# A new job list for a one-core spectral filter kernel: other order of the loads, other division of the evictions

## The chip, the core and the metric

The kernel runs on one core of a Trainium2 chip. Its time is the device time of one execution in microseconds (us); of several executions the median is given. Beside it stands one execution that the hardware profiler recorded; every duration of a single instruction comes from that one. The engines are TensorE (PE in the profile, its weight loads PEld), VectorE (DVE), ScalarE (ACT), GpSimd (POOL) and SyncE (SP), which only issues transfers. ACT and POOL issue transfers too. All transfers share 16 DMA engines.

## The reference

Two filters are applied to the same `x` (2048 x 1024, bf16). Each is a real two-dimensional FFT, a product with complex weights of 2048 x 513, and the inverse FFT. A gate, one number per row of `x`, mixes the two results.

```python
def _A_ref(x, w_r, w_i):
    B, S, D = x.shape
    X = rfft2(x.astype(float32), axes=(-2, -1))
    W = w_r + 1j * w_i
    X = X * W
    return irfft2(X, s=(S, D), axes=(-2, -1)).astype(bfloat16)
# _B_ref is the same with its own weights
g = sigmoid((x * gate_w).sum(-1, keepdims=True))
return g * _A_ref(x, A_w_r, A_w_i) + (1 - g) * _B_ref(x, B_w_r, B_w_i)
```

`B_x` is an input and is not used.

## The kernel before, in words

The transforms are cut into small DFTs that are matrix products with constant tables. The work runs in these stages; each has a name for its matmuls (ending in m) and one for the copy of the result out of PSUM (ending in e), which is called an eviction.

- **Loads.** `load.x.g.dh`: `x` comes in eight groups g, each in two halves of 256 KB. Tables: `load.E` (two parts), `F2`, `CK`, `U5`, `DI`, a 2 KB table of signs `SM`. `load.W.h.b.m.f` brings the weights of filter f for column half h and blocks b to b+m-1; each is four transfers.
- **s1 (groups 0 to 7, two column halves j).** `egen.c.v` makes signed copies of table E (v = 1 and 3 multiply with SM on DVE, 2 negates on ACT). `fold.g.k` adds, subtracts (groups 0 to 3) or reverses (groups 4 to 7) columns of `x` on DVE. `s1m.g.j` is 8 matmuls, `s1e.g.j` the eviction into buffer FR. Every later stage needs all sixteen of these evictions.
- **s2 and s4 (pairs p = 0 to 7, halves h = 1, then 0).** `s2m`, `s2e`, `s4m`, `s4e`; then `swap.p.h`, two transfers that exchange odd and even partitions of the result, and `xneg.p.h`, which multiplies the result with signs and must come after the swap has landed.
- **prod.t.h.c (t = 0 to 15, t = 2p and 2p+1).** The product with both filters' weights, on DVE. For h = 1 there are sixteen whole products. For h = 0, t = 0 to 9 are whole (c = 2); t = 10 to 15 are cut into two half products, c = 0 and c = 1. A weight block can be loaded only when the products that read the block before it in the same place are done.
- **s5 (g = 0 to 31).** `s5m.16` to `s5m.31` need all products of h = 1. `s5m.8` to `s5m.15` need the whole products of h = 0 and the halves c = 1; `s5m.0` to `s5m.7` need the whole ones and the halves c = 0. `s5e` evicts.
- **s6 and s7 (the way back).** `s6m.p.h` needs all `s5e` of its h, and table U5 scaled by the gate (`rb`, `al`). `s7m.i` (i = 0 to 15), `s7c` (ACT copies half of the result), `s7p` (two DVE additions), `fin` (two additions per i on DVE or POOL), `store`. For i = 14 and 15 the `s7p` write the output themselves and there is no `fin`.
- **The gate** beside it: `gsm`, `gse`, `rowsum`, `stm`, `zsm`, and `zse`, a sigmoid on ACT. `sig0` is a sigmoid of zeros whose only use is that it comes before. `warm` and `keep` are matmuls on zeros.

PSUM has four units of 1024 columns; a stage's matmuls take one, and its eviction gives it back.

What sets the order is a long string, `ORDER`: jobs in the order in which they are recorded. The last letter of a job names its engine or queue (a ACT, d DVE, p POOL, s SP). `Prog.add` appends each instruction to its engine's list, and derives the waits from the keys that it reads and writes. On every engine the instructions run strictly in the order of the list; nothing is reordered later. Eviction, sign, negation and addition have a helper each (lines 313 to 337), so that one line of the profile collects many jobs: L317 is every copy on ACT, L319 every copy on DVE, L322 every product, L326 and L328 signs on ACT and DVE, L332 negations on ACT, L337 every matmul, L313 every transfer, L472 the additions of `fold`, L753 `s7p`, L759 `fin`, L667 `sig0`. FR, WP and WR are the SBUF buffers, PS is PSUM.

Of the kernel before, what the change touches and what calls it, by code (L numbers as in the profile page):

```python
# [26 lines left out]
load.W.1.2.2.0.s fold.4.0.d fold.0.0.d s1m.7.0 s1m.7.1 s1m.3.1 s1e.1.1.a s1m.4.1 load.CK.s load.W.1.2.2.1.s fold.0.1.d s1e.7.0.a s1m.0.0
s1e.7.1.a s1e.3.1.a s1m.4.0 s1e.4.1.d s1m.0.1 s1m.3.0 load.R.1.0.1.1.s load.W.1.0.1.0.s s1e.0.0.a s1e.4.0.d s1m.1.0 s1e.0.1.a s1e.1.0.a
s1e.3.0.d load.GR.a keep.5.2 s2m.7.1 s2m.5.1 s2e.7.1.d s2e.5.1.d s2m.4.1 s4m.7.1 s4m.5.1 s2m.0.1 s2e.4.1.d rev s4e.7.1.a swap.7.1.a
s4e.5.1.d swap.5.1.a load.W.1.0.1.1.s s2m.6.1 s4m.4.1 s2e.6.1.d s2m.3.1 s4e.4.1.a s4m.6.1 swap.4.1.s s2e.0.1.d s2e.3.1.a s2m.1.1 s4m.3.1  # L30
xneg.7.1.d prod.14.1.2.d gwm s4e.6.1.a xneg.5.1.d load.W.1.1.1.1.s s2e.1.1.a s4e.3.1.a s4m.0.1 load.R.1.0.1.0.p load.W.1.1.1.0.s
prod.15.1.2.d gwe.a s4e.0.1.a prod.10.1.2.d xneg.4.1.d w5.0.a w5.2.a s2m.6.0 prod.11.1.2.d gsm.12.2 s2e.6.0.a swap.6.1.p gsm.8.2 s4m.1.1
prod.9.1.2.d gse.12.2.a s4e.1.1.a xneg.6.1.d load.VC.s s2m.2.1 swap.1.1.s gsm.10.2 gse.8.2.a prod.8.1.2.d prod.13.1.2.d s2e.2.1.a s4m.6.0
gse.10.2.a gsm.4.2 s4e.6.0.a swap.3.1.p prod.12.1.2.d gse.4.2.a keep.1.2 xneg.1.1.d gsm.6.2 xneg.3.1.a s4m.2.1 prod.6.1.2.d swap.0.1.p
gse.6.2.a prod.3.1.2.d gsm.0.2 w5.1.a s4e.2.1.a xneg.0.1.a swap.6.0.s gse.0.2.a w5.3.a s2m.4.0 s2m.0.0 s2m.5.0 s2e.4.0.a s2e.0.0.a gsm.14.2
gse.14.2.a s4m.4.0 prod.2.1.2.d s2e.5.0.a s4e.4.0.a prod.1.1.2.d s4m.0.0 s4m.5.0 gsm.2.2 s4e.0.0.a gse.2.2.a s2m.2.0 s2m.1.0 swap.2.1.s
prod.0.1.2.d xneg.6.0.d rowsum.0.d s4e.5.0.a prod.7.1.2.d load.W.0.2.2.1.s xneg.2.1.d rowsum.1.d s2e.2.0.a load.W.0.2.2.0.s s2e.1.0.a stm
prod.5.1.2.d swap.4.0.p load.W.0.0.1.0.s s2m.7.0 s2m.3.0 ste.a xneg.4.0.d s4m.1.0 load.W.0.0.1.1.s swap.0.0.p load.R.0.0.1.1.p prod.4.1.2.d
s4m.2.0 s2e.7.0.a s4m.7.0 xneg.0.0.d s2e.3.0.a s4e.1.0.a s4e.2.0.a s4e.7.0.a prod.8.0.2.d stx.s s5m.24 prod.12.0.0.d swap.5.0.p s5m.30
load.R.0.0.1.0.p s4m.3.0 s5e.24.a s5e.30.a rowsum.2.p stp.2.d swap.1.0.s keep.8.2 swap.7.0.s s5m.23 prod.13.0.0.d prod.9.0.2.d stp.0.d  # L40
s5m.16 swap.2.0.s keep.10.2 zsm load.W.0.1.1.1.s s4e.3.0.a prod.0.0.2.d keep.3.2 s5e.16.a xneg.1.0.d s5e.23.a s5m.31 keep.4.2 zse
prod.1.0.2.d xneg.7.0.d xneg.5.0.a s5m.27 s5e.27.a s5m.19 s5m.17 swap.3.0.p s5e.31.a prod.12.0.1.d xneg.2.0.d prod.14.0.0.d load.W.0.1.1.0.s
s5m.29 prod.11.0.0.d s5m.28 s5e.17.a prod.3.0.2.d prod.10.0.0.d keep.7.2 s5m.20 s5e.29.a s5m.21 s5e.28.a s5m.18 xneg.3.0.a s5e.19.a
prod.2.0.2.d keep.9.2 s5e.21.a stp.1.d keep.11.2 s5m.26 s5m.22 s5e.18.a zst.p keep.0.2 prod.5.0.2.d prod.4.0.2.d prod.15.0.0.d keep.2.2
prod.7.0.2.d keep.6.2 prod.6.0.2.d prod.13.0.1.d s5e.20.a s5e.26.a prod.14.0.1.d s5m.25 s5m.2 prod.11.0.1.d prod.15.0.1.d s5e.22.a c0m s5m.4
s5e.25.a s5m.1 s5e.2.a zld.s load.U5.s prod.10.0.1.d c0e.a rb.0.p s5e.4.a s5m.5 s5e.1.a s5m.3 s5m.0 s5e.5.d s5m.8 s5m.12 s5e.3.a s5e.0.d
# [789 lines left out]
```

## Time and profile before

| | us |
|---|---|
| median of 3 runs | 132.87 (132.73 to 132.93) |
| profiled execution, its own time | 132.51 |
| its span, first to last instruction | 130.7 |
| PE busy | 109.0 |
| DVE busy | 105.1 |
| ACT busy | 92.5 |
| POOL busy | 48.8 |
| mean granted TensorE clock | 0.961 |

The span is 1.8 us shorter than the profiled execution's time; what lies around it is start and end of the program. No engine is busy throughout, so shares of the span say little. The stages have different bounds: loads of `x` until 20 us, then a stretch to 91 us in which PE, ACT, DVE and the transfers feed each other, then s6 and s7. A row of the timeline gives the start, the duration, engine, line, operation, buffers, shape, count, and in brackets the idle time before it and what ended it. A row of the chain of waits gives start, duration and what the time was spent on. A row of a windows view gives the stretch, its length, each engine's busy time with the number of instructions, the granted TensorE clock, the DMA share and GB/s.

### The profile page before, as it was taken

The numbers are of one execution on the slowest core, as the hardware profiler recorded it, in microseconds if no ns is written. First come the engines' busy times: TensorE is split into PE (matmuls) and PEld (weight loads), VectorE is DVE, ScalarE is ACT, GpSimd is POOL, SyncE is SP. The second block draws the span as 40 slices with busy tenths as digits, with TensorE's granted clock in tenths as the row PEclk, the third lists the DMA queues.
The fourth block names the chain that finished last, engine by engine and source line by source line (L and its number), as shares of the span: only waits on it lengthen the run. The fifth ranks groups of instructions, "written<-read, shape, count | busy, mean of one in ns | idle before, by whom it ended". The sixth has DMA issues, their size and how long they took to land.

```text
span 130.7 us, 3713 instructions
## 1 busy us (share of the span) xinstructions
PE 109.0 (83%) x1553; PEld 87.0 (67%) x1553; DVE 105.1 (80%) x135; ACT 92.5 (71%) x121; POOL 48.8 (37%) x58
## 2 busy tenths in 40 slices
PE   6964997899999969979987835999999987999900
PEld 3343876668677756927675525999999986798300
DVE  0216858698999699973999799799979999999990
ACT  0750696521999599998999982999388995679110
POOL 3000000012170002950310000999345894999480
PEclk9997799999999999999999996799999999999995
DMA  3899999978689729999756784600000312174347
GB/s 85 284 351 351 365 327 331 294 167 209 214 222 302 245 90 242 276 346 303 230 183 176 203 271 153 291 0 5 5 0 0 115 50 86 75 278 170 115 151 259
DMA packets 27507, 25.56 MB, mean 196 GB/s; under 512 B 2834, under 2 KB 23074, under 8 KB 27234
## 3 DMA queue, kind: packets, MB, share of 16 engines
q1 hardware_dynamic: 22544, 18.41, 47.4%
q10 hardware_dynamic: 3714, 3.95, 8.9%
q0 software_dynamic: 1232, 2.96, 6.3%
q8 instruction: 12, 0.20, 0.7%
q14 instruction: 5, 0.04, 0.1%
HBM read 16.90 MB, written 4.20 MB: 161 GB/s over the span
## 4 chain that ended last, share of the span: by engine, by line
PE 37%; DMA 20%; DVE 14%; ACT 8%; SPq 7%; issue 6%; ACTq 4%; DVEq 1%
PE PS L337 37%; DMA WP<-in_A_x_dram 9%; DVE WP L322 8%; DMA WR<-in_A_w_i_dram 7%; SPq L313 7%; ACTq L313 4%; ACT WP L317 4%; DVE FR L753 4%; DMA WP<-WP 3%; ACT FR L317 2%; DVE WP L472 1%; ACT L667 1%; ACT WP L332 1%; DVEq L775 1%; DVE WR L753 0%
## 5 line engine op out<-in xcount | busy, mean ns | idle before, releaser
L317 ACT ACTIVATE WP<-PS 128x1024 bf16<-128x1024 f32 (+1 forms) x51 | 49.1, 1019 | 15.2 <-PE PS L337 14.9
L317 ACT ACTIVATE FR<-PS 128x1024 bf16<-128x1024 f32 (+1 forms) x44 | 36.2, 890 | 12.3 <-PE PS L337 9.2
L337 PE MATMUL PS<-FR,WP 128*128 128x128 bf16 (+2 forms) x384 | 32.6, 246 | 1.3 <-DVE FR L753 1.0
L337 PEld LDWEIGHTS PS<-FR,WP 128*128 128x128 bf16 x384 | 28.4, 130 | 5.1 <-DVE FR L753 1.4
L337 PE MATMUL PS<-CK,WP 128*128 128x64 bf16 x512 | 20.2, 202 | 5.4 <-DVE WP L322 4.7
L337 PEld LDWEIGHTS PS<-CK,WP 128*128 128x128 bf16 x512 | 19.3, 119 | 8.0 <-DVE WP L322 5.3
L759 POOL TENSOR_TENSOR WR<-FR 128x512 bf16<-128x512 f32 x15 | 20.4, 1369 | 7.5 <-DVE FR L753 7.2
L319 DVE CAST WP<-PS 128x1024 bf16<-128x1024 f32 x14 | 16.5, 1218 | 3.4 <-PE PS L337 3.3
L753 DVE TENSOR_TENSOR FR<-PS,FR 128x512 f32<-128x512 f32 x28 | 17.7, 678 | 1.2 <-ACT FR L317 1.0
L322 DVE TENSOR_TENSOR WP<-FR,WR 128x1024 bf16<-128x1024 bf16 (+1 forms) x18 | 14.6, 866 | 3.1 <-issue 2.2
L337 PE MATMUL PS<-F,FR 128*128 128x128 bf16 x256 | 15.9, 219 | 1.2 <-ACT FR L317 0.6
L337 PEld LDWEIGHTS PS<-F,FR 128*128 128x128 bf16 x256 | 14.7, 98 | 3.1 <-ACT FR L317 1.6
L337 PE MATMUL PS<-WP 128*128 128x256 bf16 (+1 forms) x128 | 13.4, 265 | 3.8 <-DMA WP<-in_A_x_dram 2.7
L337 PEld LDWEIGHTS PS<-WP 128*128 128x128 bf16 x128 | 10.6, 106 | 6.9 <-DMA WP<-in_A_x_dram 3.5
L322 DVE TENSOR_TENSOR WP<-WP,WR 128x2048 bf16<-128x2048 bf16 x12 | 14.3, 1217 | 0.0
L337 PE MATMUL PS<-FR 128*128 128x480 bf16 (+3 forms) x52 | 11.7, 364 | 2.7 <-ACT WP L317 1.4
L322 POOL TENSOR_TENSOR FR<-FR,F 128x1024 bf16<-128x1024 bf16 x3 | 7.3, 2438 | 16.0 <-DMA FR<-c_U 16.0
L759 DVE TENSOR_TENSOR WR<-FR 128x512 bf16<-128x512 f32 x13 | 12.6, 990 | 0.0
L313 POOL DMA_DIRECT2D FR<-FR x8 | 4.5, 565 | 17.9 <-PE PS L337 17.9
L577 POOL COPY FR<-FR 128x128 bf16<-128x128 bf16 x1 | 0.3, 292 | 27.3 <-DMA FR<-c_RG 27.3
L337 PE MATMUL PS<-WP,CK 128*128 128x512 bf16 (+4 forms) x44 | 8.7, 328 | 0.0
L337 PEld LDWEIGHTS PS<-FR 128*128 128x128 bf16 x52 | 4.2, 112 | 6.5 <-issue 1.6
(54 smaller groups left out, 88.3 us busy)
## 6 DMA issues: line engine op xcount, KB each, us to landing
WP<-in_A_x_dram ACTq DMA_DIRECT2D x9, 256.0 KB, 8.6
out_dram<-WR SPq DMA_DIRECT2D x17, 128.0 KB, 2.1
WP<-in_A_x_dram SPq DMA_DIRECT2D x7, 256.0 KB, 7.9
FR<-FR SPq DMA_DIRECT2D x8, 128.0 KB, 2.9
FR<-FR POOLq DMA_DIRECT2D x8, 128.0 KB, 5.2
FR<-c_U SPq DMA_DIRECT2D x1, 1024.0 KB, 7.2
FR<-c_DI SPq DMA_DIRECT2D x1, 1024.0 KB, 4.8
out_dram<-WR ACTq DMA_DIRECT2D x8, 128.0 KB, 2.3
```

The source lines that it names most:

```text
L313: return P.add(eng, lambda e: e.dma_start(dst, src), dma=name, **kw)
L317: P.add("act", lambda e: e.activation(dst, src, ACT.Copy), **kw)
L319: P.add(eng, lambda e: e.tensor_copy(dst, src), **kw)
L322: P.add(eng, lambda e: e.tensor_tensor(out=dst, in0=s0, in1=s1, op=ALU.mult), **kw)
L332: P.add("act", lambda e: e.activation(dst, src, ACT.Copy, scale=-1.0), **kw)
L337: P.add("pe", lambda e: e.matmul(o, lh, rh, start=first, stop=last), **kw)
L472: P.add(Q[eng], lambda e: e.tensor_tensor(out=fs, in0=xs(0, 1), in1=xs(511, -1), op=ALU.subtract if k else ALU.add), **kw)
L577: P.add("pool", lambda e: e.tensor_copy(sl(FR, GRo + 128, [(1, 128)]), sl(FR, GRo + 127, [(-1, 128)])), r=["GR"], w=["GRr"])
L667: P.add("act", lambda e: e.activation(sl(ZG, 0, [(1, 32)], np_=64), sl(FR, 20480, [(1, 32)], np_=64), ACT.Sigmoid), r=["zero", ("FR", 40), ...
L753: P.add(Q[eng], lambda e: e.tensor_tensor(out=o, in0=ps(u * 1024, [(1, 512)]), in1=eos(i), op=ALU.subtract if s else ALU.add), r=[("EO", i ...
L759: P.add(Q[eng], lambda e: e.tensor_tensor(out=od, in0=pv[0], in1=pv[1], op=ALU.subtract if s else ALU.add), r=[("PQ", i % NPQ, 0), ("PQ", ...
L775: with nc.Block() as block:
```

## The change

`ORDER` is replaced as a whole. All jobs are the same; their order and for some of them the engine or queue are new: in stage s1 to s5 ACT has 14 evictions of s2 in place of 11, 14 of s4 in place of 15, 11 of s1 in place of 12; five `xneg` in place of four; the swaps issue from POOL eleven times, from SP four times and from ACT once, in place of seven, seven and twice. In the last stage all four `rb` are on POOL, and one `s7c` is on DVE. The description with the change says that `x`'s loads were taken as one line, landings as later in saturated stretches, and GpSimd's waiting additions as ahead of VectorE's next, when the list was made. The first lines of the list, and the rest of the diff:

```diff
 ORDER = """
-load.SM.a zero load.E.1.s load.x.6.0.a warm.12x64x1.14x512x1 load.x.6.1.s load.x.2.1.a egen.1.3 egen.1.1 fold.6.0.d load.x.5.1.s
+zero load.x.3.1.a load.x.3.0.a load.SM.a load.E.1.s egen.1.1 load.x.5.1.a load.x.5.0.s load.x.2.1.s load.E.0.s warm.12x64x1.14x512x1
...
@@ def warm
-r=["zero", ("FR", 40), ("FR", 41)], w=banks(u))
+r=["zero", ("FR", 40), ("FR", 41), ("W", 3, 1)], w=banks(u))
...
@@ def sig0
-r=["zero", ("FR", 40), ("FR", 41)], w=["ZG"])
+r=["zero", ("FR", 40), ("FR", 41), ("W", 3, 1)], w=["ZG"])
```

The key `("W", 3, 1)` lets a later weight load into the same place wait until `warm` and `sig0` have read their zeros. The string has one line less, so every line of the changed kernel has a number smaller by one.

The order of the queue of ScalarE at the start, before:

```order
L313 DMA SM<-c_SM 128x4
L313 DMA WP<-in_A_x_dram 64x4x512 x3
L667 ACT_TABLE_LOAD
L667 ACTIVATE ZG<-FR 64x32
L332 ACTIVATE WP<-WP 128x1024
L313 DMA WP<-in_A_x_dram 64x4x512 x6
L317 ACTIVATE FR<-PS 128x16x16x4 x12
```

And now:

```order
L312 DMA WP<-in_A_x_dram 64x4x512 x2
L312 DMA SM<-c_SM 128x4
L312 DMA WP<-in_A_x_dram 64x4x512 x6
L331 ACT_TABLE_LOAD
L331 ACTIVATE WP<-WP 128x1024
L312 DMA WP<-in_A_x_dram 64x4x512
L312 DMA FR<-in_gate_w_dram 8x128
L312 DMA FR<-c_ALT 1x128
L312 DMA FR<-c_RG 128x32
L316 ACTIVATE FR<-PS 128x16x16x4 x11
L666 ACT_TABLE_LOAD
L666 ACTIVATE ZG<-FR 64x32
```

`SM` moved behind two halves of `x`, `sig0` (L666) moved from before the evictions of s1 to behind them, and there are two loads of the table for ScalarE's functions in place of one, since the first function on ScalarE is now a copy.

VectorE in the second half of the products of h = 1, before (TENSOR_SCALAR is `xneg`, L322 is `prod` but for the row with GSB, which is `rowsum`):

```order
L322 TENSOR_TENSOR WP<-WP,WR 128x8x64x4 x3
L328 TENSOR_SCALAR WP<-WP,SM 128x1024
L322 TENSOR_TENSOR WP<-WP,WR 128x8x64x4
L322 TENSOR_TENSOR WP<-WP,FR 128x8x64x4 x4
L328 TENSOR_SCALAR FR<-FR,SM 128x1024
L322 TENSOR_TENSOR WP<-WP,GSB 128x512
```

And now:

```order
L321 TENSOR_TENSOR WP<-WP,WR 128x8x64x4 x6
L327 TENSOR_SCALAR WP<-WP,SM 128x1024 x3
L321 TENSOR_TENSOR WP<-WP,FR 128x8x64x4 x2
L321 TENSOR_TENSOR WP<-WP,WR 128x8x64x4
L321 TENSOR_TENSOR WP<-WP,FR 128x8x64x4 x2
L321 TENSOR_TENSOR WP<-WP,WR 128x8x64x4
```

Three signs stand together ahead of the second eight products; before, one stood there.

VectorE at the end of the products of h = 0, before (128x8x32x4 is a half product, 128x8x64x4 a whole one):

```order
L322 TENSOR_TENSOR PST<-XST,W 128x64
L322 TENSOR_TENSOR WP<-FR,WR 128x8x64x4 x2
L322 TENSOR_TENSOR WP<-FR,WR 128x8x32x4
L322 TENSOR_TENSOR WP<-FR,WR 128x8x64x4 x2
L322 TENSOR_TENSOR WP<-FR,WR 128x8x32x4 x5
L319 CAST WP<-PS 128x8x128 x6
```

And now:

```order
L321 TENSOR_TENSOR WP<-FR,WR 128x8x64x4 x4
L321 TENSOR_TENSOR WP<-FR,WR 128x8x32x4 x6
L327 TENSOR_SCALAR XST<-XST,SM 128x32
L318 CAST WP<-PS 128x8x128
L321 TENSOR_TENSOR PST<-XST,W 128x64
L318 CAST WP<-PS 128x8x128 x3
```

Before, the five last halves are all c = 1, and all c = 0 are done ahead of them. Now the six last are all c = 0, and all c = 1 are done before the whole products end. TensorE now takes `s5m.9`, `12`, `13`, `10`, `11` first of h = 0; before, it took `s5m.2`, the sums for column 0, `s5m.4`.

More of the change, by code (lines that the diff above doesn't have):

```diff
@@ L27 @@
[L27 to L46, printed above, removed]
@@ new lines @@
+load.U5.s s5e.12.a s5e.10.a s5m.11 prod.11.0.0.d s5m.2 s5m.1 zld.s stp.2.d s5e.11.d s5m.5 s5m.15 rb.0.p s5e.2.a stp.1.d s5e.1.d c0m s5e.5.a
+al.0.1.p s5m.6 c0e.a s5e.15.a rb.1.p s5m.7 s5m.0 s5e.6.d s5m.8 s5e.7.a s5e.0.d al.0.0.d s5m.14 load.DI.s s5e.8.a s5m.3 s5m.4 s5e.14.a
+s6m.0.1 s5e.4.d s6m.1.1 s6e.0.1.d s5e.3.a s6m.0.0 s6e.0.0.a s6m.1.0 s7m.1 al.1.0.a rb.3.p s6e.1.1.d s7c.1.d al.1.1.a s7m.0 s7p.1.0.d
+s6e.1.0.a s7c.0.a rb.2.p s7p.1.1.d s6m.2.1 al.2.1.a s7m.2 s6m.2.0 al.2.0.a s7c.2.a al.3.0.a s7p.0.0.d fin.1.0.p s7p.0.1.d s7p.2.0.d
```

55 lines of the change are left out of this document (35 added, 20 removed).

## The prediction

> **What bounds the kernel now.** I read the chain of waits first, since the busy shares (PE 83%, DVE 80%, ACT 71%) name no single bound. Its longest pieces, in order of time:
>
> ```profile
> 7.28 12.18 DMA WP<-in_A_x_dram
> 24.76 11.95 PE PS L337 x147
> 52.31 7.16 DMA WR<-in_A_w_i_dram
> 75.73 4.10 DVE WP L322 x4
> 79.88 10.38 PE PS L337 x272
> 91.36 9.10 PE PS L337 x120
> ```
>
> The chain changes its engine in every stage: the last load of `x`, then matmuls, a weight load, the last products on DVE, the matmuls of s5, and s6. A gain in one place therefore counts only as far as the next bound lets it through. So I cut the span at three boundaries: the start of s2 (24.76), the end of s5's evictions (91.3), the end. For the two stretches behind the first boundary I read each engine's busy time:
>
> ```profile
> 24.70:91.30 66.60, 58.50 (x1029) 46.70 (x1029) 57.60 (x68) 54.79 (x73) 21.76 (x29) 0.97 0.71 209
> 95.60:127.45 31.85, 27.20 (x311) 23.20 (x308) 31.44 (x45) 22.13 (x31) 24.07 (x22) 1.00 0.29 107
> ```
>
> The busy columns are PE, PEld, DVE, ACT, POOL. From 24.7 to 91.3 ACT is idle for 66.60 - 54.79 = 11.8 us and DVE for 9.0: nobody is the bound throughout. From 95.6 to 127.45 DVE works 31.44 of 31.85 us; there it is the bound, and that stretch can only be moved, not shortened. Where ACT's 11.8 us lie:
>
> ```profile
> 24.70:40.00 15.30, 8.83 (x14) 1.00 0.81 215
> 40.00:60.00 20.00, 18.05 (x30) 1.00 0.83 252
> 60.00:77.84 17.84, 17.81 (x21) 1.00 0.77 218
> 77.84:91.30 13.46, 10.10 (x12) 0.87 0.33 124
> ```
>
> 6.5 us stand before 40, 2.0 from 40 to 60, none to 77.84, and 3.4 behind. So ACT is full for nearly 40 us, with holes at both ends.
>
> **Stage s1.** The loads of `x` stay nine on ACT's queue and seven on SP's, with E's two parts at SP's first and fourth place as before; only which group stands where is new, and `SM` moved from ACT's first place to behind two halves of `x`. The folds show when groups arrive, since each waits for its transfers:
>
> ```profile
> 3.60 0.88 DVE L328 TENSOR_SCALAR WP<-WP,SM 128x1024 bf16<-128x1024 bf16 x2 [3.60 <-DMA SM<-c_SM]
> 6.63 0.43 DVE L319 COPY WP<-WP 128x1024 bf16<-128x1024 bf16 x1 [2.16 <-DMA WP<-in_A_x_dram]
> 9.91 0.69 DVE L472 TENSOR_TENSOR WP<-WP 128x1024 bf16<-128x1024 bf16 x1 [2.85 <-DMA WP<-in_A_x_dram]
> 11.42 8.36 PE L337 MATMUL PS<-WP 128*128 128x256 bf16 x72 [2.49 <-DMA WP<-in_A_x_dram]
> 12.98 1.29 DVE L472 TENSOR_TENSOR WP<-WP 128x1024 bf16<-128x1024 bf16 x2 [0.16 <-DMA WP<-in_A_x_dram]
> 18.36 0.43 DVE L319 COPY WP<-WP 128x1024 bf16<-128x1024 bf16 x1 [0.68 <-DMA WP<-in_A_x_dram]
> 19.48 1.29 DVE L472 TENSOR_TENSOR WP<-WP 128x1024 bf16<-128x1024 bf16 x2 [0.69 <-DMA WP<-in_A_x_dram]
> 12.00:12.50 0.50, 0.50 (x4) 0.31 (x3) 0.50 (x2) 0.00 (x0) 0.00 (x0) 0.50 1.10 344
> ```
>
> ACT's first `x` is there at 6.63, its third at 9.91, its eighth at 18.36, its ninth at 19.48. A new order cannot move these. `SM` now follows the second, between 6.63 and 9.91; I take the middle, 8.2. DVE then does a sign, a fold and a sign (0.44, 0.65, 0.44) and at 9.9 the fold of group 5 (0.43), so that TensorE begins at 10.4: 1.0 us before its second start of now, 11.42, but with all sixteen units left instead of fourteen. It was idle as long as before, so I expect the half clock that the last row shows (0.50) again. In before it holds to about 14.8. A unit of group 4 to 7 takes 0.87 at full clock (the 15 matmuls of 1.81 us in the rows right below, less the last one's tail), the others half of that; by 14.8 four units are done, and DVE starts on `s1e.5.0`. From there DVE has five evictions, four additions and two copies left: 5 x 1.18 + 4 x 0.645 + 2 x 0.43 = 9.3, with 1.18 from four in 4.74. None of its folds waits: group 0 is wanted at 18.9 and there at 18.36, group 4 at 20.2 and there at 19.48. So s2 begins at 24.1 in place of 24.76: **-0.65**. Bounds: without the half clock DVE waits for group 0 at 18.36, and 1.29 + 0.43 + 3.54 later it is 23.6, or -1.1; with `SM` at 9.9, everything behind is 1.7 later, of which folds hide some: +1.0 at most.
>
> ```profile
> 7.12 1.81 PE L337 MATMUL PS<-WP 128*128 128x256 bf16 x15 [0.18 <-DVE WP L319]
> 25.85 4.74 DVE L319 CAST WP<-PS 128x1024 bf16<-128x1024 f32 x4 [1.19 <-PE PS L337]
> ```
>
> **From s2 to the end of s5, by ACT.** These rows price what moves, and the two holes at the start:
>
> ```profile
> 3.58 1.28 ACT L667 ACT_TABLE_LOAD   x1 [3.58 <-issue]
> 4.87 0.23 ACT L667 ACTIVATE ZG<-FR 64x32 bf16<-64x32 bf16 x1
> 28.50 1.02 ACT L317 ACTIVATE WP<-PS 128x1024 bf16<-128x1024 f32 x1 [3.81 <-PE PS L337]
> 32.19 1.02 ACT L317 ACTIVATE WP<-PS 128x1024 bf16<-128x1024 f32 x1 [2.67 <-PE PS L337]
> 43.27 1.15 ACT L326 ACTIVATE WP<-WP,SM 128x1024 bf16<-128x1024 bf16 x1 [0.74 <-issue]
> 73.16 4.68 ACT L317 ACTIVATE WP<-PS 128x1024 bf16<-128x1024 f32 x5
> 80.96 10.35 ACT L317 ACTIVATE WP<-PS 128x1024 bf16<-128x1024 f32 x11 [3.12 <-PE PS L337]
> ```
>
> ACT gets three evictions of s2 more and one of s4 less (0.94 each, from five in 4.68): +1.9. One `xneg` more: +1.15. One copy of 16 columns less, taken at 0.23 like the row of that size: -0.2. The second table load and `sig0`, which now stand between the last eviction of s1 and the first of s2: +1.28 + 0.23 = +1.5. The first load, now ahead of `egen.1.2`, is hidden by the wait for `x` until 9.9. Sum: +4.3, so 54.8 + 4.3 = 59.1 us of work. Counted from 24.0, ACT would end at 83.1 without any idle.
>
> Its idle time: the holes of 3.81 and 2.67 at the start are now filled by the table load with `sig0` and by two s2 evictions (1.5 + 1.9 = 3.4), which leaves 3.1 of 6.5. The 2.0 from 40 to 60 stay. The hole of 3.12 at 80.96 came from TensorE's wait for products; it should go (next part), and 0.2 of that stretch is left. 3.1 + 2.0 + 0.2 = 5.3, and 83.1 + 5.3 = 88.4 in place of 91.3: **-2.9**, with the -0.65 of s1 inside.
>
> The Trainium skill, "ScalarE: Activation LUTs", section "What ACT_TABLE_LOAD costs", speaks against this term: it gives about 1283 ns for the load and a drain of about 1380 ns, some 2.66 us for every switch to another set. The trace agrees with the first number (1.28) but shows no drain: the next instruction starts at 4.87, right behind it; whether one comes with a switch no row here shows, since before loads one table only. By the page the sum would be 1.4 us less favourable, -0.5 in place of the -1.9 below.
>
> **Does DVE let it through?** These are its waits in that stretch, and the last products:
>
> ```profile
> 46.06 0.49 DVE L328 TENSOR_SCALAR WP<-WP,SM 128x1024 bf16<-128x1024 bf16 x1 [1.46 <-DMA WP<-WP]
> 57.44 0.49 DVE L328 TENSOR_SCALAR FR<-FR,SM 128x1024 bf16<-128x1024 bf16 x1 [0.97 <-DMA FR<-FR]
> 61.63 1.83 DVE L322 TENSOR_TENSOR WP<-FR,WR 128x2048 bf16<-128x2048 bf16 x2 [2.17 <-issue]
> 74.59 8.24 DVE L322 TENSOR_TENSOR WP<-FR,WR 128x2048 bf16<-128x2048 bf16 x10 [0.91 <-DVE PST L322]
> 79.88 1.04 PE L337 MATMUL PS<-CK,WP 128*128 128x64 bf16 x16 [3.56 <-DVE WP L322]
> ```
>
> Before, DVE ends its products at 74.59 + 8.24 = 82.8. Up to there it loses three casts of s2 and one `xneg` and gains one cast of s4, one of s5 (`s5e.24`) and a small copy: -3.54 - 0.48 + 2.36 + 0.25 = -1.4. With s1's -0.65 it ends at 80.8, even if every wait above stays. The last ten products are four whole ones and six halves, about 1.14 and 0.61 each. Now the six halves c = 0 stand last and five s5 groups need none of them; these open 6 x 0.61 = 3.7 before 80.8, at 77.1, and not at 79.88. TensorE's hole of 3.56 and the half clock behind it go, and ACT, which ends h = 1 at about 78.0 by its account, finds `s5m.9` done.
>
> **What is late next: swaps.** POOL issues eleven of them, not seven. The rows of the transfers:
>
> ```profile
> FR<-FR SPq DMA_DIRECT2D x8, 128.0 KB, 2.9
> FR<-FR POOLq DMA_DIRECT2D x8, 128.0 KB, 5.2
> WP<-WP SPq DMA_DIRECT2D x6, 128.0 KB, 2.6
> WP<-WP POOLq DMA_DIRECT2D x6, 128.0 KB, 3.8
> ```
>
> A swap from POOL lands 1.2 to 2.3 us later than one from SP. Queued behind a waiting `xneg` on DVE are all later products: behind `xneg.6.0`, whose swap moves from SP to POOL, stands `prod.15.0.1`, and for the products s5 waits. The three signs that now stand together want three swaps at once. Cost: 0 if all are early, 2.3 if one is late in full. I take **+1.0**, nearer to the small end, as the waits of 1.46 and 0.97 above are of that size and the new order gives most swaps more time.
>
> **s6 and s7.** Counted in the new list, DVE has 32 additions of L753 and 13 of L759 as before, loses one `rb` and gains one `s7c`, both 0.6 to 0.7: 0. POOL keeps 15 additions. It gets one `rb` more, but loses three of its four `al`. ACT gets three `al` more, and has room. The last unit is again one without `fin`, and `fin.13` the last addition. I take **0**; bounds -0.4, DVE's idle time there, and +0.7 for one more addition of that size that is waited for.
>
> Sum: -2.9 + 1.0 + 0 = **-1.9** against the profiled 132.51 (span 130.7): 130.6. The median of the runs shown lies 0.36 above the profiled execution, which gives **131.0**.
>
> **Rivals.**
> - *Nothing new is late* (0.14). For it: DVE's account holds with all old waits. Then the +1.0 falls away: 130.0.
> - *The weights decide* (0.15). The chain has 7.16 us of a weight transfer at 52.31, and DVE's largest wait, 2.17, follows it. Those loads start when the first eight products end, and these begin with a swap, as before. If they land no earlier, DVE ends at 82.8 again, five s5 groups open at 79.1 in place of 79.88, and the gain is 0.7: 132.2. Against it: SP has the same transfers with fewer swaps between them.
> - *ACT becomes the bound, slower* (0.20). ACT has 4.3 us more to do in a stretch where it was idle for 11.8. From an idle time of 91.3 - 83.1 = 8.2 us on, the change loses. If the holes at the start stay, because TensorE and the swaps and not ACT set the pace there, only the 3.12 goes: 8.7, or +0.5; with a late swap of 1.0 on top +1.5. In the middle +1.0: 133.9. For it: 17.81 of 17.84 us busy up to 77.84.
> - *The table switch costs twice its row* (0.06). If ACT stands still after the second load for as long as the load took, 1.28, the first eviction of s2 comes that much later, and the swap and products behind it: 131.0 + 1.3 = 132.3. Against it: the one load of the trace is followed at once, at 4.87. This is the drain of the Trainium skill, "ScalarE: Activation LUTs", weighed above.
> - *`x` does not come sooner* is part of the forecast: its queues move the same bytes in the same places.
>
> **How the numbers follow.** The forecast has 0.45, with a range of its own from 130.3 to 131.9. About 0.2% (0.27 us) is what a measurement of this kernel can tell from none. Faster: 0.45 + 0.14 and most of 0.15 and 0.06, 0.74; within: 0.05; slower: 0.21. The range reaches from 129.3 (no late swap, and s1 and s7 at their good bounds in part) to 133.6, which leaves out about half of the slower case.
>
> **What would show it.** TensorE's first matmul of s1 at 10.4 and the first of s2 at 24.1; a second table load directly behind the last s1 eviction, lasting 1.28, with or without a gap; no hole on ACT near 78, and clock 1.00 from 79 to 83; the last `s5e` at 89.4; DVE full from 93 on. The forecast is wrong if ACT shows holes of more than 8 us from 24 to the last `s5e`, or if DVE waits for a swap of POOL by more than 2 us, or for a weight as long as now.

## The result and the profile after

The changed kernel takes 142.94 us (median of four executions, 142.74 to 143.78); the kernel before, on the same chip, 132.80 (132.70 to 132.93). The ratio is 1.0775, 95% interval 1.073 to 1.082: slower by 7.8%, where 131.0 was forecast with a range to 133.6. The profiled execution took 142.81, with a span of 140.6 and a mean clock of 0.937. On some of the chips that were used below, single executions of the kernel before came out 3 to 6% longer than its others; the ratios leave such executions out, the medians of the table below keep them.

In the line numbers of the changed kernel the products are L321, evictions on ScalarE L316 and on VectorE L318, matmuls L336.

VectorE's timeline has the row that answers the 74.59 / 8.24 of before. The last ten products, four whole ones and six halves, took twice as long, and they began 1.2 us later:

```profile
75.77 16.38 DVE L321 TENSOR_TENSOR WP<-FR,WR 128x2048 bf16<-128x2048 bf16 x10 [4.12 <-DMA WR<-in_A_w_i_dram]
```

Two things are in this row: a wait of 4.12 us for a weight in front of it (0.91 before), and 8.1 us more of work. The groups of instructions, by shape, tell which of the ten grew. First before, then after; L321/L322 on VectorE with 128x1024 are the twelve half products, with 128x2048 out of FR and WR six of the whole ones, and on GpSimd (POOL) they are `rb`:

```profile
L322 DVE TENSOR_TENSOR WP<-FR,WR 128x1024 bf16<-128x1024 bf16 x12 | 7.8, 687 | 0.0
...
L322 DVE TENSOR_TENSOR WP<-FR,WR 128x2048 bf16<-128x2048 bf16 x6 | 7.2, 1224 | 3.1 <-issue 2.2 <-DVE PST L322 0.9
```

```profile
L321 DVE TENSOR_TENSOR WP<-FR,WR 128x1024 bf16<-128x1024 bf16 x12 | 15.9, 1363 | 0.5 <-DVE WP L318 0.5
...
L321 POOL TENSOR_TENSOR FR<-FR,F 128x1024 bf16<-128x1024 bf16 x4 | 9.9, 2501 | 11.3 <-DMA F<-zd 11.3
...
L321 DVE TENSOR_TENSOR WP<-FR,WR 128x2048 bf16<-128x2048 bf16 x6 | 7.0, 1221 | 4.1 <-DMA WR<-in_A_w_i_dram 4.1
```

The whole products are what they were (1221 ns, 1224 before). The half products have a mean of 1363 ns instead of 687: 15.9 - 7.8 = 8.1 us. Beside them stands GpSimd, in its own timeline:

```profile
80.69 2.32 POOL L321 TENSOR_TENSOR FR<-FR,F 128x1024 bf16<-128x1024 bf16 x1 [11.32 <-DMA F<-zd]
83.07 0.95 POOL L318 COPY FR<-FR 128x512 bf16<-128x512 bf16 x1
83.99 7.61 POOL L321 TENSOR_TENSOR FR<-FR,F 128x1024 bf16<-128x1024 bf16 x3
```

`rb.0`, a copy (`al.0.1`) and the three other `rb` fill 80.69 to 91.60, almost without a gap. The six halves end at 75.77 + 16.38 = 92.15. Taken one by one, the first half (80.32 to 81.01) has its old length; of the five others four took 2.6 us, each beside one `rb`, and one 1.1 us beside the copy. Each of these five ends 0.55 us after the GpSimd instruction beside it. So VectorE and GpSimd took turns: one instruction of the one, one of the other. The recorded lengths of both hold the wait for the other: the last three `rb` read 2.56 each, and 2.13 where they are alone (e1). So a meeting with `rb` lengthens a half by 1.9 us, a little less than `rb`'s own time; four of these and the 0.4 at the copy are the 8.1 us.

What waited for it, on TensorE and ScalarE:

```profile
80.46 4.46 PE L336 MATMUL PS<-CK,WP 128*128 128x64 bf16 x80 [6.31 <-DVE WP L321]
92.20 0.99 PE L336 MATMUL PS<-CK,WP 128*128 128x64 bf16 x15 [7.29 <-DVE WP L321]
```

```profile
93.28 1.03 ACT L316 ACTIVATE WP<-PS 128x1024 bf16<-128x1024 f32 x1 [7.18 <-PE PS L336]
...
96.30 5.02 ACT L316 ACTIVATE WP<-PS 128x128 bf16<-128x128 f32 x6 [0.29 <-PE PS L336]
```

TensorE does the five s5 groups that need no half c = 0, and then waits 7.29 us for VectorE. The last `s5e` ends at 96.30 + 5.02 = 101.32 instead of 91.31. The chain of waits, from 71 on, is now this (start, duration, what):

```profile
71.63 3.95 DMA WR<-in_A_w_i_dram
...
76.91 15.24 DVE WP L321 x9
...
92.20 10.81 PE PS L336 x240
```

Its three pieces are the weight, the products, s5. From 101.32 to the end of the span it is 140.6 - 101.3 = 39.3 us, against 130.7 - 91.3 = 39.4 before: the whole loss lies ahead of the last `s5e`. The windows by stage (columns PE, PEld, DVE, ACT, POOL, clock, DMA share, GB/s) say the same, and that the loss lies behind 75.8:

```profile
24.40:40.00 15.60, 15.51 (x209) 12.14 (x210) 11.74 (x12) 12.75 (x17) 5.00 (x9) 1.00 0.73 204
40.00:60.00 20.00, 19.17 (x326) 14.91 (x324) 18.41 (x23) 19.09 (x31) 9.63 (x19) 1.00 0.97 288
60.00:75.80 15.80, 11.97 (x210) 8.72 (x208) 10.79 (x16) 15.80 (x19) 0.63 (x1) 0.89 0.67 185
75.80:101.40 25.60, 13.65 (x297) 13.50 (x298) 22.82 (x19) 10.98 (x13) 10.85 (x5) 0.73 0.22 81
```

ACT is idle for 15.60 - 12.75 = 2.85, then 0.91, then 0.0 us, and in the last stretch for 14.6.

### The profile page after: what moved, and what is told of

The parts are those of the page before. It is cut to its first block, busy times and chain, and to the rows that moved or that the text cites. A ratio compares the mean times of both kernels' runs of the same rounds, so it can differ in the third digit from the quotient of the medians.

```text
span 140.6 us, 3712 instructions
## 1 busy us (share of the span) xinstructions
PE 110.6 (79%) x1553; PEld 88.5 (63%) x1553; DVE 112.1 (80%) x134; ACT 96.1 (68%) x125; POOL 51.5 (37%) x63
## 4 chain that ended last, share of the span: by engine, by line
PE 24%; DVE 19%; ACT 18%; DMA 15%; issue 8%; SPq 7%; ACTq 5%; DVEq 1%
PE PS L336 24%; DVE WP L321 12%; DMA WP<-in_A_x_dram 9%; ACT FR L316 9%; SPq L312 7%; ACT WP L316 6%; DVE FR L752 5%; ACTq L312 5%; DMA FR<-in_B_w_i_dram 3%; DMA WR<-in_A_w_i_dram 3%; ACT WP L325 2%; DVE WR L758 1%; ACT FR L331 1%; DVE WR L752 0%; DVEq L774 0%
## 5 line engine op out<-in xcount | busy, mean ns | idle before, releaser
L316 ACT ACTIVATE WP<-PS 128x1024 bf16<-128x1024 f32 (+1 forms) x53 | 50.9, 1020 | 21.6 <-PE PS L336 21.6
L316 ACT ACTIVATE FR<-PS 128x1024 bf16<-128x1024 f32 (+1 forms) x42 | 35.2, 893 | 9.4 <-PE PS L336 8.3
L336 PE MATMUL PS<-CK,WP 128*128 128x64 bf16 x512 | 22.7, 213 | 16.1 <-DVE WP L321 14.3
L336 PE MATMUL PS<-FR,WP 128*128 128x128 bf16 (+2 forms) x384 | 32.8, 245 | 2.4 <-DVE FR L752 1.9
L336 PEld LDWEIGHTS PS<-CK,WP 128*128 128x128 bf16 x512 | 21.7, 122 | 19.0 <-DVE WP L321 15.4
L336 PEld LDWEIGHTS PS<-FR,WP 128*128 128x128 bf16 x384 | 28.1, 130 | 6.7 <-DVE FR L752 2.8
L321 DVE TENSOR_TENSOR WP<-FR,WR 128x1024 bf16<-128x1024 bf16 (+1 forms) x18 | 22.6, 1316 | 4.6 <-DMA WR<-in_A_w_i_dram 4.1
L318 DVE CAST WP<-PS 128x1024 bf16<-128x1024 f32 x12 | 14.3, 1219 | 6.5 <-PE PS L336 6.5
L336 PE MATMUL PS<-F,FR 128*128 128x128 bf16 x256 | 15.6, 219 | 0.8 <-ACT FR L316 0.8
L336 PEld LDWEIGHTS PS<-F,FR 128*128 128x128 bf16 x256 | 14.7, 98 | 2.2 <-ACT FR L316 1.2
L321 DVE TENSOR_TENSOR WP<-WP,WR 128x2048 bf16<-128x2048 bf16 x12 | 14.1, 1221 | 0.3 <-ACT WP L325 0.3
L336 PE MATMUL PS<-FR 128*128 128x480 bf16 (+3 forms) x52 | 12.9, 397 | 1.8 <-POOL FR L374 1.3
L336 PE MATMUL PS<-WP 128*128 128x256 bf16 (+1 forms) x128 | 11.6, 246 | 3.3 <-DVE WP L318 2.1
L321 POOL TENSOR_TENSOR FR<-FR,F 128x1024 bf16<-128x1024 bf16 x4 | 9.9, 2501 | 11.3 <-DMA F<-zd 11.3
L336 PEld LDWEIGHTS PS<-WP 128*128 128x128 bf16 x128 | 9.7, 98 | 5.5 <-issue 2.3
L312 POOL DMA_DIRECT2D WP<-WP x10 | 5.6, 560 | 14.7 <-DVE WP L318 10.4
L327 DVE TENSOR_SCALAR WP<-WP,SM 128x1024 bf16<-128x1024 bf16 x9 | 4.1, 483 | 8.5 <-DMA SM<-c_SM 7.8
L312 POOL DMA_DIRECT2D FR<-FR x12 | 6.5, 543 | 7.8 <-PE PS L336 7.6
L336 PEld LDWEIGHTS PS<-FR 128*128 128x128 bf16 x52 | 4.5, 117 | 6.4 <-issue 3.2
```

The source lines that it names most:

```text
L312: return P.add(eng, lambda e: e.dma_start(dst, src), dma=name, **kw)
L316: P.add("act", lambda e: e.activation(dst, src, ACT.Copy), **kw)
L318: P.add(eng, lambda e: e.tensor_copy(dst, src), **kw)
L321: P.add(eng, lambda e: e.tensor_tensor(out=dst, in0=s0, in1=s1, op=ALU.mult), **kw)
L327: P.add(eng, lambda e: e.tensor_scalar(out=dst, in0=src, scalar1=SM[:, col:col + 1], scalar2=None, op0=ALU.mult), **kw)
L336: P.add("pe", lambda e: e.matmul(o, lh, rh, start=first, stop=last), **kw)
```

## The experiments

Theory A: a half product that runs while GpSimd works on SBUF takes as long as GpSimd's instruction; the change brought `rb` and the half products together, and the 8 to 10 us that this makes are the main cost. The rivals (the weight, other parts of the change) stand in each expectation. All runs in one table; "products" is the end of VectorE's last product of h = 0, "last s5e" the end of s5, both from the profiled execution, whose span stands behind them. Times with the number of executions.

| run | time, us | kernel before beside it | products | last s5e | span |
|---|---|---|---|---|---|
| before | 132.80 (4) | | 82.8 | 91.3 | 130.7 |
| after | 142.94 (4) | 132.80 | 92.1 | 101.3 | 140.6 |
| e1 `rb` held back | 134.06 (4) | 132.83 | 83.5 | 92.4 | 131.7 |
| e2 two `rb` held back | 137.12 (1) | 132.83 | 85.8 | 95.6 | 134.9 |
| e3 two swaps to GpSimd | 135.74 (1) | 132.83 | 82.2 | 94.3 | 133.6 |
| e6 `rb` as a copy | 137.81 (1) | 132.83 | 87.2 | 96.3 | 135.6 |
| e4 U5 first, in before | 133.11 (9) | 133.21 | 82.2 | 90.8 | 130.2 |
| e5 e1 and e3 together | 130.94 (4) | 133.21 | 79.8 | 88.5 | 127.8 |
| e7 halves moved | 134.71 (4) | 133.21 | 79.2 | 92.6 | 132.0 |
| e9 e5, products and casts shifted | 129.70 (6) | 133.21 | 79.5 | 89.2 | 128.5 |
| e10 collision made in before | 138.22 (2) | | 89.7 | 98.7 | 138.2 |
| e11 e10, `rb` held back | 134.24 (2) | | 86.2 | 93.5 | 133.0 |

In all twelve rows the span is the last `s5e` plus 39.3 to 39.5. Nothing that was moved ahead of that point changed the length of what comes behind it.

### e1: `rb` waits for the products

```diff
 def rb(c, eng):
-    mult(..., r=["U5", "SI"], a=[("RP", c)])
+    mult(..., r=["U5", "SI"] + [("prod", 0, v) for v in range(2) if c in (0, 1, 2, 3)], a=[("RP", c)])
```

> The changed kernel, but the four scalings rb on GpSimd wait until all products of h = 0 are done; nothing else moves. Theory A (the half products c = 0 on VectorE stand still while an rb on GpSimd works, both with two operands in SBUF): the six halves take 0.69 each again, the last ends at 84.1 in place of 92.1, TensorE has no hole of 7.3 before s5m.2, and the time falls by 8 to 10: 133 to 135. Rival B (the halves are slow because U5 and DI land in SBUF at that time, or because of where they read and write): the halves stay near 2.6, time within 0.5 of 142.9. Rival C (the weight wait of 4.12 at 71.6 is the cause and the rest only follows it): time within 1 of 142.9.

The time fell from 142.94 to 134.06, 8.9 us, inside A's range (the kernel before takes 132.80 and 132.83 beside the two). VectorE's row, GpSimd's row and the group of the halves:

```profile
75.21 8.25 DVE L321 TENSOR_TENSOR WP<-FR,WR 128x2048 bf16<-128x2048 bf16 x10 [4.83 <-ACT WP L316]
```

```profile
83.64 2.13 POOL L321 TENSOR_TENSOR FR<-FR,F 128x1024 bf16<-128x1024 bf16 x1 [14.94 <-DVE XST L327]
...
83.99 1.22 DVE L318 CAST WP<-PS 128x1024 bf16<-128x1024 f32 x1 [0.39 <-PE PS L336]
```

```profile
L321 DVE TENSOR_TENSOR WP<-FR,WR 128x1024 bf16<-128x1024 bf16 x12 | 7.7, 685 | 0.0
```

The ten products take 8.25 us again, the halves 685 ns. `rb.0` takes 2.13 alone; and VectorE's cast at 83.99, which reads PSUM and runs beside it, has its usual 1.22. B and C fall: `DI` was still on its way into SBUF (issued at 79.87, landed at 84.61) and the halves beside it took their old time, and the weight wait is still there (4.83, though the row names ScalarE as what ended it). What is left of the loss, 134.06 against 132.83, is no larger than the scatter of single executions (132.13 to 135.51, and 130.80 to 134.03 for the kernel before).

### e2: only `rb.2` and `rb.3` wait

```diff
-... if c in (0, 1, 2, 3)]
+... if c in (2, 3)]
```

> As the kernel before it in this list, but only rb.3 and rb.2 wait for the products; rb.0 and rb.1 stay where they are. Theory A: two halves cost about 2.6, the others 0.69 (one may be lengthened by al.0.1, a copy, as now); the last half ends about 3.9 earlier than in the changed kernel, at 88.2; time near 139. Rival B: no change.

```profile
73.22 12.54 DVE L321 TENSOR_TENSOR WP<-FR,WR 128x2048 bf16<-128x2048 bf16 x10 [3.39 <-DMA WR<-in_A_w_i_dram]
```

12.54 us: 4.3 more than in e1 and 3.8 fewer than in the changed kernel. Two halves took 2.6 us beside `rb.0` and `rb.1`, one 1.1 beside the copy, the others 0.69. The products end at 85.8 and not at the 88.2 that was expected, as the ten began 2.6 us earlier in this execution (73.22 against 75.77); their length is what A gave. The cost goes with the number of GpSimd instructions that meet a half.

### e3: two swaps from SP to GpSimd, `rb` untouched

```diff
-... swap.0.0.s ... swap.2.0.s ... load.W.0.1.1.1.s
+... swap.0.0.p ... swap.2.0.p ... load.W.0.1.1.1.s
```

> The changed kernel with swap.0.0 and swap.2.0 issued by GpSimd in place of SyncE, so that SyncE issues the last weights of h = 0 about 3 us sooner. rb is not touched. Theory A: VectorE's wait of 4.12 for these weights falls below 1; the whole products end at 77.2, the six halves by 80.9, and since U5 and the gate's table still land near 80.5, at most one half meets an rb: last half at 81 to 83, time 131 to 134. Rival B: halves 2.6 each wherever they stand, last half at 92 - 3.3 = 89, time near 139.5. Rival C: time falls by the 3.3 of the wait alone, 139.5.

```profile
73.95 8.24 DVE L321 TENSOR_TENSOR WP<-FR,WR 128x2048 bf16<-128x2048 bf16 x10
82.11 2.12 DVE L327 TENSOR_SCALAR XST<-XST,SM 128x32 bf16<-128x32 bf16 x1
84.14 1.21 DVE L318 CAST WP<-PS 128x1024 bf16<-128x1024 f32 x1
85.27 1.72 DVE L321 TENSOR_TENSOR PST<-XST,W 128x64 bf16<-128x64 bf16 x1
```

```profile
80.59 3.60 POOL L321 TENSOR_TENSOR FR<-FR,F 128x1024 bf16<-128x1024 bf16 x1 [9.61 <-DMA F<-zd]
```

The weight wait is gone, and the last ten products begin 1.8 us earlier than in the changed kernel (73.95, 75.77). When `rb.0` comes at 80.59, one half is running and two are left, and this time VectorE's go first. The ten take 8.24 in all, and GpSimd is the one that waits (3.60 instead of 2.13). Then the roles change: VectorE's `stp.2`, a multiplication of 32 numbers per partition that takes 0.22 elsewhere, takes 2.12 and ends with `rb.0`; `stp.1` takes 1.72 beside the next `rb`. Both stand in front of casts, so part of the gain is lost: 135.74, above the 131 to 134 that A gave, and well below the 139.5 of B and C. The halves are short without any change to `rb`, and A gets wider: also a tiny instruction on VectorE waits out a whole one of GpSimd. (The first stage of this execution ended 1.0 us later than in the changed kernel's.)

### e6: `rb` as a copy in place

```diff
-    mult(Q[eng], o, o, sl(F2, ...), r=["U5", "SI"], a=[("RP", c)])
+    copy(Q[eng], o, o, r=["U5", "SI"], a=[("RP", c)])
```

> The changed kernel with each rb a copy of U5 in place (one operand) in place of the product with the gate; the scaling by the gate is left out. Theory A in its narrow form (it is the two SBUF operands on GpSimd): the halves take at most what al.0.1, a copy, cost now (1.1 in place of 0.69), last half near 85.5, time near 136. Theory A in its wide form (any work of GpSimd in SBUF holds up VectorE's products): the halves take as long as the copy, some 1.2 to 2 each, last half at 87 to 92. Rival B: no change, 2.6.

```profile
L321 DVE TENSOR_TENSOR WP<-FR,WR 128x1024 bf16<-128x1024 bf16 x12 | 11.5, 999 | 0.0
...
L318 POOL COPY FR<-FR 128x1024 bf16<-128x1024 bf16 x4 | 6.2, 1586 | 10.0 <-DMA F<-zd 10.0
```

The copy reads one operand where `rb` reads two (the scaling by the gate falls away with it). Its mean is 1.59 in place of 2.50, and the halves beside it became shorter by about as much: 1.5 instead of 2.6. So a second operand on GpSimd's side is not needed: a copy inside SBUF holds the halves up as well, by 0.8 us each. That is A in its wide form; the narrow one gave 1.1 at most. Work of GpSimd that does not read SBUF was not tried.

### e4: U5 ahead of zld, in the kernel before

```diff
-... s5e.2.a zld.s load.U5.s prod.10.0.1.d
+... s5e.2.a load.U5.s zld.s prod.10.0.1.d
```

> The kernel before, with one thing of the change put into it: U5 is loaded ahead of zld. In the kernel before U5 landed at 81.73 and rb.0 ran from 81.80, when DVE had two of its five last half products left; issued first (some 72.0) U5 should land near 79 and zld near 80.5, so that rb.0 is ready at about 80 with five halves (79.74 to 82.83) still to come. Theory A (a half product beside GpSimd's rb takes as long as rb): one or two halves of 2.6 us and one of 1.1, products end 2 to 4.5 us later (85 to 87.3), time 134.5 to 137. Theory B (the change's other moves are what hurt, the weight wait above all): products end at 82.8 and the time stays at 132.5 to 133.3.

```profile
81.71 2.53 POOL L322 TENSOR_TENSOR FR<-FR,F 128x1024 bf16<-128x1024 bf16 x1 [16.72 <-DVE WP L322]
```

Inconclusive: the edit did not bring `rb.0` forward. U5 could not be issued before 72.99, zld then took 3.8 us to issue and landed at 81.56, and `rb.0` began at 81.71, as before (81.80), with no half after it. The traced execution took 131.97, and the ratio is 0.994 (0.988 to 0.999). The nine executions lie between 131.28 and 142.39; whether the two instructions met in the longer ones is open, since none of these was traced. It was replaced by e10.

### e10 and e11: the collision made in the kernel before

```diff
-... prod.13.0.1.d ... prod.14.0.1.d ... prod.11.0.1.d prod.15.0.1.d ... s5e.2.a ... prod.10.0.1.d
+... s5e.2.d prod.13.0.1.d prod.14.0.1.d prod.11.0.1.d prod.15.0.1.d prod.10.0.1.d
```

> The kernel before, with its last five half products behind the cast s5e.2, which VectorE now does instead of ScalarE; rb untouched. The cast (near 81.0 to 82.2) reads PSUM and lets rb.0 begin at its old time (81.8), so that the halves come while GpSimd works. Theory A (a half product beside GpSimd's work takes as long as that work): halves of 2.4 to 2.6 us beside each rb and 1.1 beside each al, products end 89 to 92 instead of 82.8, last s5e 95 to 98, time 136.5 to 139. Theory B (what the change did elsewhere made its halves long): five halves of 0.69 from 82.2, products end 85.2, last s5e 91.5 to 93, time 133 to 134.5.

e11 is the same order, with `rb` held back as in e1.

> The same order of products and casts as in the run that makes the collision, and rb waits for all products, as a control. Theory A: halves at 0.69, products end 85.2, rb.0 from there at 2.13, last s5e 91.5 to 93.5, time 133 to 135, some 3 to 4 us less than with rb left free. Theory B: no difference between the two but rb's later start; 133 to 134.5 in both.

e10, VectorE and GpSimd, then e11:

```profile
81.95 7.79 DVE L322 TENSOR_TENSOR WP<-FR,WR 128x1024 bf16<-128x1024 bf16 x5
```

```profile
82.18 2.45 POOL L322 TENSOR_TENSOR FR<-FR,F 128x1024 bf16<-128x1024 bf16 x1 [16.15 <-PE PS L337]
84.69 0.96 POOL L319 COPY FR<-FR 128x512 bf16<-128x512 bf16 x1
```

```profile
83.05 3.10 DVE L322 TENSOR_TENSOR WP<-FR,WR 128x1024 bf16<-128x1024 bf16 x5
```

Five halves take 7.79 us beside GpSimd and 3.10 when `rb` is held. The last `s5e` of e10 is at 98.7, that of e11 at 93.5, the spans 138.2 and 133.0: 5.2 us between the two traces, 4.7 of them in the five halves, in a kernel that has nothing else of the change. The two executions of each are 136.45 and 139.99, and 133.62 and 134.86: the medians are 4.0 apart, and the traced one of e10 is the longer of its two. (Of the kernel before there were three executions on this chip, 132.38, 139.48 and 140.05, too scattered for a ratio; the pair is compared by its own traces.) The median of e10 lies in A's range and its traced execution, 139.99, 1 us above; e11 lies inside.

### e5: `rb` held back and the two swaps on GpSimd

The edits of e1 and e3 together.

> The kernel after, with rb waiting for DVE's products and swap.0.0 and swap.2.0 issued by GpSimd, so that both SP's weight loads and rb are out of the way. With rb alone held back the time was 134.1 and DVE still waited 4.83 us for the weight. Theory A: whole products end near 78.6, halves at 0.69 each near 82.2, s5m.2 right behind them; the 16 casts from there are what lasts, last s5e 91 to 92, time 132.5 to 133.5, so the weight wait of 4.8 us was worth about 1 us once rb is away. Theory C (the weights decide what is left): the whole wait comes back, time 129.5 to 130.5.

```profile
71.52 8.23 DVE L321 TENSOR_TENSOR WP<-FR,WR 128x2048 bf16<-128x2048 bf16 x10
```

No wait in front, 8.23 for ten. The products end 3.7 us earlier than in e1 (79.8 against 83.5) and the last `s5e` 3.9 us earlier. The time is 130.94 (129.27 to 132.21), 1.7% under the 133.21 of the kernel before. My expectation, that the casts would be what lasts and the wait be worth about 1 us, was wrong: of the 4.8 us, 3.9 came back at the last `s5e` and 3.1 in the time (the two runs are from different chips). That is nearer to theory C, which gave 129.5 to 130.5. SP's rows show how the swaps held the weight up; first of the changed kernel, then of e5:

```profile
62.01 1.25 SPq L312 DMA_DIRECT2D XST<-XST  x2
63.36 3.08 SPq L312 DMA_DIRECT2D FR<-FR  x4
66.56 0.65 SPq L312 DMA_DIRECT2D WR<-in_B_w_r_dram  x1
```

```profile
61.19 1.26 SPq L312 DMA_DIRECT2D XST<-XST  x2
62.54 0.65 SPq L312 DMA_DIRECT2D WR<-in_B_w_r_dram  x1
```

The four transfers of the two swaps took 3.08 us of SP's queue to issue, between `stx` and the weight. Without them the weight's first transfer goes out at 62.54 in place of 66.56, and its last part landed at 71.2 in place of 75.6. Of these 4.0 us at the issue the swaps make 3.2; `stx` itself was issued 0.8 us earlier in this execution.

### e7: the six halves moved into the weight wait

```diff
-... prod.0.0.2.d prod.7.0.2.d ... prod.15.0.0.d prod.12.0.0.d prod.10.0.0.d prod.14.0.0.d prod.13.0.0.d ... prod.11.0.0.d
+... prod.0.0.2.d prod.15.0.0.d prod.12.0.0.d prod.10.0.0.d prod.14.0.0.d prod.13.0.0.d prod.11.0.0.d prod.7.0.2.d ...
```

> The kernel after, with the six half products of columns 0 moved ahead of prod.7.0.2, into the 4.12 us in which DVE waited for the weight; rb, its engine and its wait untouched. Theory A: halves of 0.69 us each from 71.6 to 75.3, whole products to 80.4 as now, rb.0 at about 80.7 beside nothing that reads two operands of SBUF except the small stp products (up to 2 us each); s5m.2 about 84 instead of 92.2, last s5e 91.5 to 93 instead of 101.3, time 133 to 134.5. Theory D (rb holds up DVE's casts from PSUM as well): casts beside rb take 2 us and more, last s5e 96 to 98, time 137 to 139.

```profile
74.53 4.63 DVE L321 TENSOR_TENSOR WP<-FR,WR 128x2048 bf16<-128x2048 bf16 x4 [0.35 <-ACT WP L316]
79.08 0.23 DVE L327 TENSOR_SCALAR XST<-XST,SM 128x32 bf16<-128x32 bf16 x1
83.71 1.22 DVE L318 CAST WP<-PS 128x1024 bf16<-128x1024 f32 x1 [4.41 <-PE PS L336]
```

`rb` is untouched, on its engine, without a new wait; each takes 2.1 to 2.2 us and meets no half any more, only `stp.1`, which it holds up (1.37). 134.71, ratio 1.012 (1.006 to 1.018), 0.2 above A's range: 8.2 us of the loss are gone by the order alone. The products end at 79.2, 3.7 us ahead of the kernel before, and still the last `s5e` is 1.3 us later than there: now no group of s5 can begin before the last whole product, and VectorE then stands idle for 4.41 us, as its first cast is the fifth in line. Theory D, that casts are held up too, falls: the casts beside `rb` take 1.22.

### e9: a version that beats both

e5, and `stp.2`, `prod.15.0.0`, `prod.14.0.0`, `stp.1` ahead of `prod.3.0.2`, where VectorE waited for a moment; `s5e.13` and `s5e.14` from ScalarE to VectorE, `al.0.0` the other way.

```diff
-... prod.13.0.1.d prod.3.0.2.d
+... prod.13.0.1.d stp.2.d prod.15.0.0.d prod.14.0.0.d stp.1.d prod.3.0.2.d
-... s5e.13.a ... al.0.0.d ... s5e.14.a
+... s5e.13.d ... al.0.0.a ... s5e.14.d
```

> The kernel after, with rb waiting for the products, swap.0.0 and swap.2.0 on GpSimd, two of the six halves and both stp ahead of prod.3.0.2 (where DVE waited 1.70 us once those swaps were on GpSimd), and the casts of s5 split 9 to 7 between ScalarE and VectorE instead of 11 to 5. Theory A: whole products end 77.5 to 78.5, the last four halves 80 to 81, 16 casts at 0.92 and 1.13 us on two engines from there, last s5e 88.5 to 90 against 91.3 in the kernel before, time 130.3 to 132, faster than the kernel before. If the end of the casts is set by something else (PE's s5m, rb), the last s5e stays at 91 to 92.5 and the time at 132.5 to 134.

```profile
72.50 7.03 DVE L321 TENSOR_TENSOR WP<-FR,WR 128x2048 bf16<-128x2048 bf16 x8
```

129.70 (median of six), ratio to the kernel before 0.969 (0.963 to 0.975): faster by 3.1%, and slightly under the expected 130.3 to 132. Against e5 the step is small and is not shown: the traced e5 has its last `s5e` at 88.5, the traced e9 at 89.2.

## Why the prediction was wrong, point by point

- **The term that failed: the last products.** "The last ten products are four whole ones and six halves, about 1.14 and 0.61 each." The whole ones were. The halves, 3.7 us by that count, took from 80.32 to 92.15, 11.8 us. That is 8.1 us of the 11.9 by which the forecast was short. e1, e2, e6, e7, e10 and e11 show the cause: five of the six met an instruction of GpSimd. The prediction saw that GpSimd gets one `rb` more, and counted it only as work on GpSimd ("POOL keeps 15 additions. It gets one `rb` more"); what `rb` does to VectorE had no term and no rival. The trace of before had the sign, in GpSimd's timeline, two rows that I had not read against each other:

```profile
81.80 3.03 POOL L322 TENSOR_TENSOR FR<-FR,F 128x1024 bf16<-128x1024 bf16 x1 [16.01 <-DMA FR<-c_U]
...
85.46 2.15 POOL L322 TENSOR_TENSOR FR<-FR,F 128x1024 bf16<-128x1024 bf16 x1
```

  The same instruction takes 3.03 us beside VectorE's last two halves and 2.15 behind them. The Trainium skill, "SBUF — State Buffer", section "Who interferes with whom", has this rule: a VectorE instruction with two SBUF inputs contends with a GpSimd instruction that reads SBUF, and the contention is an exclusive lock on the port pair that the two engines share. The trace agrees, 0.69 against 2.6. By the same section of the Trainium skill an instruction with at most one SBUF input, outside the modes that use two ports, does not contend; the casts, whose only input is PSUM, keep 1.22 beside `rb` (e1). The prediction had not drawn on it.
- **Whole products end at 77.1.** They ended at 75.77 + 4 x 1.14 = 80.3, through the wait of 4.12 for a weight; the forecast had left that wait at 0.91, as it was in before. They were late by 3.2 us against the forecast; with the 8.1 of the halves that is 11.3 of the 11.9. This is the rival "the weights decide", and it was half right: the mechanism was there, and e5 against e1 gives its size, 3.1 us in the times and 3.9 at the last `s5e`, where 1.2 was allowed for. The argument against it, "fewer swaps between them", is true and did not help. SP's rows of before, to be held against those under e5:

```profile
61.82 3.75 SPq L313 DMA_DIRECT2D FR<-FR  x6
66.08 0.66 SPq L313 DMA_DIRECT2D WR<-in_B_w_r_dram  x1
```

  Three swaps stood ahead of the last weight there, two stand there now, and the weight was issued at 66.08 before and at 66.56 now. Its last part landed at 74.51 before and at 75.58 now. VectorE, though, was done with what stands ahead at 71.65 instead of 73.67. So 2.0 us of the longer wait are VectorE's own gain, which the weight did not follow, and 1.1 are the later landing.
- **The two are linked.** By the forecast the halves would have ended at 80.8, and `rb.0` began at 80.69 in the changed kernel: in that execution it was the late weight that pushed the halves into `rb`. e3, which mends only the weight, has its halves short and takes 135.74; e1, which mends only `rb`, 134.06; e5, with both, 130.94. That they would always have missed each other is not shown: in e2 `rb.0` began at 78.19.
- **ACT's account from s2 on was near up to 75.8.** Idle time at the start: 3.1 forecast, 2.85 measured; from 40 to 60: 2.0 and 0.91; then none. The last entry, 0.2 for the stretch behind, became 14.6. ACT did not become the bound.
- **Swaps, +1.0.** VectorE's waits for swaps in the changed kernel are 0.58 and 0.27, together 0.85, where before they were 1.46 and 0.97. By this count the term should have been -1.6.
- **The second table load.** No gap: the load starts when the last eviction of s1 is done, takes 1.28, and the next instruction follows it at once; the first eviction of s2 too. ScalarE's timeline:

```profile
23.34 1.02 ACT L316 ACTIVATE FR<-PS 128x1024 bf16<-128x1024 f32 x1 [1.86 <-PE PS L336]
24.39 1.28 ACT L666 ACT_TABLE_LOAD   x1
25.68 0.23 ACT L666 ACTIVATE ZG<-FR 64x32 bf16<-64x32 bf16 x1
25.82 1.91 ACT L316 ACTIVATE WP<-PS 128x1024 bf16<-128x1024 f32 x2
```

  The drain of about 1380 ns that the Trainium skill gives ("ScalarE: Activation LUTs", "What ACT_TABLE_LOAD costs") does not show here, with a switch this time.
- **Stage s1, -0.65.** `SM` was there at 7.83 (8.2 forecast) and TensorE's first matmul came at 10.24 (10.4 forecast), but what followed was not as forecast: no half clock came (1.00 throughout), and s2 began at 24.49. "A new order cannot move these", said of the landings of `x`, did not hold for the last one: it landed at 20.54, where before it was 19.45.

```profile
7.83 0.49 DVE L327 TENSOR_SCALAR WP<-WP,SM 128x1024 bf16<-128x1024 bf16 x1 [7.83 <-DMA SM<-c_SM]
```

```profile
10.24 8.49 PE L336 MATMUL PS<-WP 128*128 128x256 bf16 x96 [1.90 <-DVE WP L318]
...
24.49 2.67 PE L336 MATMUL PS<-F,FR 128*128 128x128 bf16 x45 [0.78 <-ACT FR L316]
```

  Over all traces here s2 begins between 23.90 and 25.45 with the new first stage (eight traces, mean 24.6), and between 24.76 and 25.10 with the old one (four traces, mean 24.9). The last `x` lands between 19.95 and 21.50 with the new one and between 19.45 and 19.79 with the old one, and s2 follows it by 3.9 us in all eight and by 5.3 in all four (24.49 - 20.54 and 24.76 - 19.45 are the first of each). So the new order made the end of the stage 1.4 us shorter, and its last load lands 1.1 us later: the term is -0.3, and smaller than its scatter from one execution to the next.
- **s6 and s7, 0.** Right: 39.3 us from the last `s5e` to the end, 39.4 before, and the same in every run of the table.
- **The slower side.** It had 0.21, by ACT becoming the bound. It came by a mechanism that stood nowhere in the list. Without the two things that failed, with `rb` held back and two swaps on another queue, the list takes 130.94 (e5), where 131.0 was forecast. That it comes so near is partly luck: errors in the rest of the sum (the swaps, s1) cancel, and single executions of e5 lie from 129.27 to 132.21.

Still open: what is left between e7's 134.71 and e5's 130.94 is told by their traces (the begin of s5), not by a run of its own.

## What to carry to other kernels

Before an instruction on GpSimd that works on SBUF is moved, look at what VectorE does at that moment: beside casts out of PSUM it cost nothing here, beside products of two SBUF operands each meeting added about GpSimd's own time (2.6 us in place of 0.69, where `rb` alone takes 2.13). An instruction whose length differs from one occurrence to the next in the same trace (3.03 and 2.15) can be the sign of such a meeting, and it is to be read before any sum is made with its mean. And a transfer that the path waits for is priced with everything that stands ahead of it in its queue: two swaps ahead of a weight took 3.08 us of SP's queue here.
